# A spectral filter and a gated FFN on one core: stage A of batch 1 through folded chunks on VectorE and GpSimd, x in one lasting buffer

## The chip, the cores and the metric

The kernel runs on one core of one Trainium2 chip. The core's engines run side by side, each through its own queue of instructions in order: TensorE (PE, with its weight loads as PEld), VectorE (DVE), ScalarE (ACT), GpSimd (POOL) and the sync engine (SP). DMAs are issued from the queues of SP, ACT and POOL. The metric is the device time of one execution in microseconds (us); the span is the part of it between the first and the last recorded instruction.

## The reference, cut to what matters

```python
def _attn_ref(x, filt_r, filt_i):            # x: (8, 3008, 256) float32
    X = np.fft.rfft(x, axis=1)
    F = (filt_r + 1j * filt_i)[None, :, :]
    y = np.fft.irfft(X * F, n=x.shape[1], axis=1)
    return y.astype(np.float32)

def _moe_ref(x, w_gate, w_val, w_out):       # x: (24064, 256), d_ff 1536
    gate = np.maximum(x @ w_gate, 0.0)
    val = x @ w_val
    return (gate * val @ w_out).astype(np.float32)

# reference: _moe_ref(_attn_ref(x, filt_r, filt_i).reshape(8 * 3008, 256), w_gate, w_val, w_out)
```

Each of the 8 batches is filtered along its 3008 positions in the frequency domain, and every position then goes through a gated FFN.

## The kernel before

A transform of length 3008 is split as 94 x 32. Position s is written s = 32 n1 + n2, and a batch goes through three stages of matmuls:

- Stage A transforms over n1 for every n2. Its result goes to a DRAM buffer Abuf[b] and is gathered from there, with another order of rows, into the tile "at" (load_at, load_at_tiled).
- Stage B transforms over n2 (fwd, line 356), multiplies with the filter tiles Ftr and Fti (product, line 369, four products of 128 x 512 for each of six groups i) and transforms back (inv, line 383). Its result goes to Dbuf[b] and is read back as dC (load_d, line 423).
- Stage C transforms back over n1 and gives the FFN's input yT for a block of 512 positions (item_c, line 444; one half is copied by ScalarE, the other by VectorE).

The FFN runs over 47 blocks of 12 steps. A step multiplies with a slice of w_val and w_gate (gv, line 461: four matmuls of 512 columns, a cast vsb on ScalarE, prod on VectorE) and with a part of w_out for the block before (o_part, line 478). The stages of the coming batches are hung into these steps with at_step(s, f), which runs f in step s of the program; the order in every queue is the order of the program.

Stage A exists in two forms. The whole form (items_a, line 269) multiplies x as it is, with 94 rows of n1 in the partitions of XF, by WA in float32: 16 items of 512 columns for a batch, each with a cast on ScalarE (asb). Batches 0 and 1 use it. The folded form is for batches 2 to 7: load_chunk (line 291) brings a quarter of the batch's x into XP[j] from the GpSimd queue, once in order and once reversed; fold_chunk (line 304) forms sums and differences of rows that mirror each other, in six float32 instructions on GpSimd, two of 1024 columns and four of 512; tiled_a (line 317) multiplies them in 16 small matmuls, four at a time beside each other, and casts the result half on ScalarE and half on VectorE. A tile "fold" with two buffers holds part of a fold until its tiled_a has read it.

Ahead of the FFN stands the prologue, in this order of the program (lines 514 to 586):

- x of batch 0 is loaded into XF, the filters into Ftr and Fti from GpSimd's queue. The rows 64 to 95 of their last two groups come by loads of their own (load_own_filters, line 226).
- Stage A of batch 0 in 16 items, and the gather of at (SP's queue).
- make_back_t (line 186, casts I2t on VectorE) and make_back_u (line 199, reads I2t on TensorE, casts I2u on ScalarE) make the tables of the inverse, three calls each, with warm(6) behind each call: six matmuls on junk data, which keep TensorE busy. Between the two, place_filter(0) (line 233) copies filter rows to the partitions 32 further on, four copies of Ftr on VectorE; after them place_own, place_filter(1) and place_nyq.
- x of batch 1 is loaded into XF on SP's queue (line 557). GpSimd waits for at (hold_gpsimd, line 255: a tiny copy that holds its queue) and loads the first halves of w_val and w_gate.
- first_b (line 406) is stage B of batch 0. It calls amid(i) after each group: a short warm for i < 2, six items of batch 1's stage A after that. POOL_U (line 344) lists the products that go to GpSimd, each behind a copy xs on ScalarE.
- The spectra of batch 0 are read back, the second weight halves and w_out are loaded, the ten other items of batch 1's stage A run, and item_c(0, h) makes the first yT.

XF, WA, the junk tile and the other tiles of the pool "pro" are given up at prologue.close(); the pool "fs" of the FFN, with XP in it, takes their place. XP is cleared on GpSimd at step 2.

Of the kernel before, what the change touches and what calls it, by code (L numbers as in the profile page):

```python
# [120 lines left out]
def kernel(  # L121
# [32 lines left out]
    Abuf = [dram.tile([NROW * N2, D], BF16, name=f"Abuf{b}") for b in range(B)]  # L154
    Dbuf = [dram.tile([NROW * N2, D], BF16, name=f"Dbuf{b}") for b in range(B)]

    XF = [pro.tile([128, NX2 * D], FP32, name=f"XF{c}") for c in range(N2 // NX2)]
    WA = pro.tile([128, NROW], FP32)
    WF = consts.tile([128, 4, 32], FP32)
    M1 = consts.tile([NROW, N1], BF16)  # L160
# [79 lines left out]
    def place_nyq():  # L240
        for (src, dst), n in zip(FILT, nyq):
            nc.vector.tensor_copy(dst[96:97, NG - 1, :], n)
# [58 lines left out]
                              _ap(x, ((b * N1 + 46 + 47 * i) * N2 + 2 * j) * D,  # L301
                                  [[8 * D, 4], [-N2 * D, 32], [1, 512]]))

    def fold_chunk(b, j):

        xp = XP[j]
        t = fs.tile([128, 2, 512], FP32, tag="fold", bufs=2, name="fold")
        tt = nc.gpsimd.tensor_tensor
        tt(t, xp[:, 0:2], xp[:, 2:4], op=ALU.add)  # L309
        tt(xp[:, 2:4], xp[:, 0:2], xp[:, 2:4], op=ALU.subtract)  # L310
        tt(xp[:, 0], t[:, 0], t[:, 1], op=ALU.add)
        tt(t[:, 0], t[:, 0], t[:, 1], op=ALU.subtract)
        tt(t[:, 1], xp[:, 2], xp[:, 3], op=ALU.add)
        tt(xp[:, 2], xp[:, 2], xp[:, 3], op=ALU.subtract)
        fold[b, j] = (xp[:, 0], t[:, 0], t[:, 1], xp[:, 2])
# [25 lines left out]
                              _ap(Abuf[b], (48 * (rr % 2) + 24 * (rr // 2)) * N2 * D,  # L341
                                  [[D, 32], [N2 * D, 24], [1, D]]))

    POOL_U = ((0, 0), (0, 1), (1, 1), (2, 0), (2, 1), (3, 1), (4, 0))
    ats = {}

    def load_at(b, c):
# [159 lines left out]
    def warm(n, cols=512):  # L507

        psJ = ps.tile([128, 512], FP32, tag=fft_tag(True), name="psJ")
        for i in range(n):  # L510
            nc.tensor.matmul(psJ[:, :cols], junk[:, 0:128], junk[:, :cols], start=True, stop=True)
# [27 lines left out]
            load_at(0, 0)  # L539
    for c in range(1, 4):  # L540
        load_at(0, c)
    for i in range(3):
        make_back_t(i)
        warm(6)
    for half in range(2):
        for a in range(2):
            place_filter(0, a, half, nc.vector.tensor_copy)
    for i in range(3):
        make_back_u(i)
        warm(6)  # L550
    warm(6)
    place_own()
    for half in range(2):
        for a in range(2):
            place_filter(1, a, half, nc.vector.tensor_copy if a or not half else nc.scalar.copy)
    place_nyq()
    load_x(1, nc.sync, ((0, 0, 2 * q), (0, 2 * q, 4 * q), (1, 0, 4 * q)))

    early = items_a(1)

    def amid(i):
        if i < 2:
            warm(3, 256)
        else:
            for _ in range((1, 1, 2, 1, 1)[i - 2]):
                next(early)()

    hold_gpsimd(ats[0][0:32, NG - 1, 0:8])
    load_vg(0, DFF // 2)
    turn["tags"], turn["side"] = ("fft", "psv", "psg"), "pso"  # L570
    first_b(amid)
    turn["tags"], turn["side"] = ("fft", "psv", "psg", "pso"), None
    load_d(0, 0, 2)
    nc.gpsimd.dma_start(pro.tile([1, D], BF16, tag="last", bufs=1, name="last"),
                        _ap(Dbuf[0], (N2 * NROW - 1) * D, [[D, 1], [1, D]]))
    load_vg(DFF // 2, DFF)
    load_at(1, 0)
    for i, f in enumerate(early):
        f()
        if i == 5:  # L580
            load_at(1, 1)
    for h in range(2):
        item_c(0, h)
    hold_gpsimd(yTs[0][:, 0, 0:8])
    load_o()
    prologue.close()
    fs = ctx.enter_context(tc.tile_pool(name="fs", bufs=2))
    XP = []

    def clear_chunks():  # L590
        for i in range(4):
            XP.append(fs.tile([128, 4, 512], FP32, tag=f"XP{i}", bufs=1, name=f"XP{i}"))
            nc.gpsimd.memset(XP[i], 0.0)

    turn["tags"] = ("fft",)
    side = {}

    def at_step(s, f):
        side.setdefault(s, []).append(f)
# [1 line left out]
    for s, z in ((9, 2), (14, 3)):  # L601
        at_step(s, lambda z=z: load_d(0, z, z + 1))
    C_AT = (8, 10)
    at_step(2, clear_chunks)
    for b in range(1, B):
        end = (b * S // W - 1) * NFT + C_AT[0] - 5
        if b == 1:
            for c in range(2, 4):
                at_step(c - 2, lambda c=c: load_at(1, c))
        else:  # L610
            for j, e in enumerate((-74, -69, -64, -57)):
                l = (22, 34, 34, 46)[j] if b == 2 else end - 113 + NFT * j

                def next_x(b=b, j=j, l=l):
                    hold_gpsimd(yTs[l // NFT + 1][:, 0, 0:8])
                    load_chunk(b, j)
                    if j:
                        fold_chunk(b, j - 1)
                    if j == 3:
                        fold_chunk(b, j)  # L620
                at_step(l, next_x)
                at_step(end + e, lambda b=b, j=j: tiled_a(b, j))
            at_step(end + e + 4, lambda b=b: load_at_tiled(b))
        for i in range(7):
            l = -35 + 5 * i if b == 1 else -40 + 6 * i
            if i < 6:
                at_step(end + l, lambda b=b, i=i: fwd(b, i))
                for h in range(4):
                    at_step(end + l + h, lambda b=b, i=i, h=h: product(b, i, h // 2, h % 2))
            if i > 0:  # L630
                at_step(end + l, lambda b=b, i=i: inv(b, i - 1, ("psv", "psg")))
        at_step(end - 2, lambda b=b: load_d(b))
    prev = None
    for k in range(NB):
        prods = []
# [39 lines left out]
```

## Time and profile before

| what | value |
|---|---|
| median of 3 runs | 903.96 us (903.3 to 905.86) |
| the profiled execution | 903.85 us, of which the span is 902.1 us |
| fwd of batch 0, first matmul | 35.11 us |
| last cast of the first B ends | 53.8 us |
| first matmul of the FFN | 63.02 us |
| first matmul with w_out (block 1) | 76.22 us |

Busy time of the engines by stretch of the span, in us:

| stretch | PE | DVE | ACT | POOL | granted clock |
|---|---|---|---|---|---|
| 0 to 35 (loads, stage A of batch 0, tables) | 29.61 | 12.57 | 14.12 | 10.94 | 1.00 |
| 35 to 53.8 (first B) | 15.97 | 12.41 | 14.27 | 9.66 | 0.91 |
| 53.8 to 63 (rest of batch 1's stage A) | 8.04 | 0.69 | 6.29 | 2.02 | 1.00 |
| 63 to 76.2 (block 0) | 12.16 | 8.69 | 7.83 | 8.89 | 1.00 |
| 76.2 to 902.1 (blocks 1 to 46) | 811.33 | 534.42 | 459.61 | 327.50 | 1.00 |

The span is one execution's; the times outside it (1.75 us) are the start and the end. A line of the timeline gives the start, the length, the engine and line, the operation with its output and input, how many of it were merged, and in brackets how long the engine was idle before it and what released it. A letter q behind an engine (SPq, POOLq) stands for its queue of DMA issues.

### The profile page before, as it was taken

How to read it: one execution, taken by the hardware profiler on the slowest of the kernel's cores; microseconds unless marked ns; L12 is line 12 of the kernel's file. 1: busy time of each engine (PE TensorE's matmuls, PEld its weight loads, DVE VectorE, ACT ScalarE, POOL GpSimd, SP SyncE). 2: the span in 40 equal slices, each digit the busy share in tenths (PEclk: the TensorE clock that was granted, in tenths of full speed). 3: DMA queues.
4: the chain of work that ended last, by engine and by line, in shares of the span. 5: the costliest groups of instructions: out<-in, count | busy, mean ns of one | idle time of the engine just before them, and what ended most of it. 6: DMA issues, size and time to landing. Idle time of an engine off the chain costs nothing.

```text
span 902.1 us, 19072 instructions
## 1 busy us (share of the span) xinstructions
PE 877.1 (97%) x7089; PEld 511.1 (57%) x7210; DVE 568.8 (63%) x872; ACT 502.1 (56%) x891; POOL 359.0 (40%) x352
## 2 busy tenths in 40 slices
PE   7899999999999999999999999999999999999997
PEld 2335555566555665566655666556655566666664
DVE  2636766577765776667766677657766577655553
ACT  3475555456655555555655565655565555555552
POOL 4332398228670486515773167801868000000000
PEclk9999999999999999999999999999999999999999
DMA  9978359524465344663365434763446512321111
GB/s 248 295 204 168 106 144 188 111 81 114 137 150 123 96 132 122 143 132 105 98 162 136 107 100 105 182 126 87 112 140 148 119 30 82 90 63 36 37 34 50
DMA packets 113759, 109.18 MB, mean 121 GB/s; under 512 B 20290, under 2 KB 98370, under 8 KB 113026
## 3 DMA queue, kind: packets, MB, share of 16 engines
q1 hardware_dynamic: 90662, 80.40, 34.8%
q0 software_dynamic: 22176, 26.01, 11.9%
q10 hardware_dynamic: 828, 1.54, 0.5%
q8 instruction: 57, 0.93, 0.5%
q14 instruction: 36, 0.29, 0.1%
HBM read 61.93 MB, written 49.81 MB: 124 GB/s over the span
## 4 chain that ended last, share of the span: by engine, by line
PE 78%; POOL 5%; DMA 5%; DVE 4%; ACT 4%; issue 3%; SPq 1%; POOLq 0%; DVEq 0%
PE psG L467 24%; PE psO L486 23%; PE psV L467 22%; DVE prod L472 4%; ACT vsb L470 3%; PE psF L323 3%; PE psD L394 2%; PE psX L364 1%; DMA WgT<-in_moe_w_gate_dram 1%; PE psY L451 1%; DMA XP<-in_x_dram 1%; PE psA L276 1%; POOL XP L296 1%; DMA XF<-in_x_dram 1%; POOL fold L309 1%
## 5 line engine op out<-in xcount | busy, mean ns | idle before, releaser
L472 DVE SCALAR_TENSOR_TENSOR prod<-psG,vsb 128x512 bf16<-128x512 f32 x564 | 389.3, 690 | 265.6 <-ACT vsb L470 256.2
L470 ACT CAST vsb<-psV 128x512 bf16<-128x512 f32 x564 | 332.2, 589 | 267.8 <-PE psV L467 165.2
L467 PE MATMUL psG<-yT,WgT 128*128 128x512 bf16 x1107 | 330.8, 379 | 7.1 <-DMA WgT<-in_moe_w_gate_dram 0.6
L486 PE MATMUL psO<-WoT,prod 128*128 128x256 bf16 x2256 | 336.4, 273 | 1.1
L467 PE MATMUL psV<-yT,WvT 128*128 128x512 bf16 x1030 | 315.3, 380 | 1.2 <-ACT yT L456 1.2
L486 PEld LDWEIGHTS <-prod 128*128 128x128 bf16 x2256 | 220.6, 98 | 143.4
L467 PEld LDWEIGHTS <-WgT 128*128 128x128 bf16 x1128 | 109.9, 98 | 136.5 <-issue 2.2
L467 PEld LDWEIGHTS <-WvT 128*128 128x128 bf16 x1128 | 98.4, 98 | 42.3 <-issue 30.9
L258 POOL CAST scr<-yT 128x8 f32<-128x8 bf16 x25 | 4.7, 190 | 266.9 <-ACT yT L456 266.9
L492 ACT COPY osb<-psO 128x512 f32<-128x512 f32 x92 | 53.9, 586 | 27.4 <-PE psO L486 25.7
L380 DVE TENSOR_TENSOR tt<-psX,Ftr 128x512 bf16<-128x512 f32 x96 | 65.1, 683 | 4.6 <-PE psX L364 4.5
L309 POOL TENSOR_TENSOR fold<-XP 128x1024 f32<-128x1024 f32 x24 | 56.5, 2355 | 23.2 <-PE psF L323 23.0
L380 DVE TENSOR_TENSOR uu<-psX,Fti 128x512 bf16<-128x512 f32 x89 | 60.7, 681 | 0.0
L401 ACT CAST dsb<-psD 128x512 bf16<-128x512 f32 x96 | 51.5, 589 | 12.5 <-PE psD L394 12.4
L310 POOL TENSOR_TENSOR XP<-XP 128x1024 f32<-128x1024 f32 x24 | 56.3, 2347 | 1.9
L296 POOL DMA_DIRECT2D XP<-in_x_dram x96 | 56.2, 590 | 0.9 <-issue 0.5
L330 DVE CAST asb<-psF 128x512 bf16<-128x512 f32 x48 | 30.9, 687 | 20.5 <-PE psF L323 15.5
L330 ACT CAST asb<-psF 128x512 bf16<-128x512 f32 x48 | 25.8, 589 | 30.2 <-PE psF L323 30.2
L456 ACT CAST yT<-psY 128x512 bf16<-128x512 f32 x47 | 27.5, 586 | 24.8 <-PE psY L451 24.2
L458 DVE CAST yT<-psY 128x512 bf16<-128x512 f32 x47 | 32.0, 681 | 10.8 <-PE psY L451 10.8
L451 PE MATMUL psY<-M,dC 96*128 96x94 bf16 (+18 forms) x604 | 37.5, 198 | 0.1
L451 PEld LDWEIGHTS <-dC 96*128 96x128 bf16 x604 | 34.5, 97 | 3.6 <-issue 1.2
(66 smaller groups left out, 478.1 us busy)
## 6 DMA issues: line engine op xcount, KB each, us to landing
at<-Abuf SPq DMA_DIRECT2D x32, 384.0 KB
dC<-Dbuf SPq DMA_DIRECT2D x64, 192.0 KB
XP<-in_x_dram POOLq DMA_DIRECT2D x48, 256.0 KB, 6.0
Dbuf<-dsb SPq DMA_DIRECT2D x23, 512.0 KB
XP<-in_x_dram POOLq DMA_DIRECT2D x96, 96.0 KB, 2.7
Abuf<-asb SPq DMA_DIRECT2D x96, 96.0 KB
out_dram<-osb SPq DMA_DIRECT2D x70, 94.0 KB
XF<-in_x_dram SPq DMA_DIRECT2D x15, 256.0 KB
```

The source lines that it names most:

```text
L296: nc.gpsimd.dma_start(xp[r:r + 24, 0:4:2, :], _ap(x, (b * N1 * N2 + o) * D, [[N2 * D, 24], [47 * N2 * D, 2], [1, 512]]))
L309: tt(t, xp[:, 0:2], xp[:, 2:4], op=ALU.add)
L310: tt(xp[:, 2:4], xp[:, 0:2], xp[:, 2:4], op=ALU.subtract)
L330: copy(asf[:, :, q, :], banks[q])
L380: nc.vector.tensor_tensor(p, psX, filt, op=ALU.mult)
L401: nc.scalar.copy(dsb[:, a, o:o + 2, :], psD[a])
L451: nc.tensor.matmul(psY[:, o:o + w], dCs[b, n2 // 8][:, n2 % 8, h * 128:(h + 1) * 128], M1[:, n1:n1 + w], start=True, stop=True)
L467: nc.tensor.matmul(pt[:, :W], w[:, h, ft * 128:(ft + 1) * 128], yt[:, h, :], start=(h == 0), stop=(h == 1))
L470: nc.scalar.copy(vsb, psV[:, :W])
L472: nc.vector.scalar_tensor_tensor(prod, in0=psG[:, :W], scalar=0.0, in1=vsb, op0=ALU.max, op1=ALU.mult)
L486: nc.tensor.matmul(psO[:, t % 2], prods[ft][:, t * 128:(t + 1) * 128], WoT[:, ft, :], start=(ft == 0), stop=(ft == NFT - 1))
L492: copy(osb[:, t0 % 2:t % 2 + 1], psO[:, t0 % 2:t % 2 + 1])
```

## The change

Batch 1 takes the folded form as well. Its x is loaded into XF, which now lasts for the whole kernel: XD is XF seen as four rows of 1024 columns, and the four chunks XP[j] are views of XD. load_pairs brings two chunks at a time: the rows in order from SP's queue, the reversed rows from GpSimd's. fold_chunk takes an engine and a pool: chunks 0 and 1 of batch 1 are folded on VectorE behind the first B, chunk 2 on GpSimd at the same place, chunk 3 on GpSimd behind the loads of the weights. tiled_a(1, 0) runs ahead of the FFN, the three others in steps 1, 3 and 10 of it, and the gather of at for batch 1 in step 11. The tile "fold" moves from the pool fs to sb, with a buffer of its own in pro for chunk 0. In the prologue place_filter(0) stands ahead of make_back_t, and the seven warm(6) are together behind place_nyq. amid runs warms of 256 columns alone, POOL_U has six products instead of seven, and the clearing of XP and two holds of GpSimd's queue go. Stage B of batch 1 starts two steps later and reads back one step later.

```diff
@@ -154,7 +154,9 @@
     Abuf = [dram.tile([NROW * N2, D], BF16, name=f"Abuf{b}") for b in range(B)]
     Dbuf = [dram.tile([NROW * N2, D], BF16, name=f"Dbuf{b}") for b in range(B)]
 
-    XF = [pro.tile([128, NX2 * D], FP32, name=f"XF{c}") for c in range(N2 // NX2)]
+    XF = [consts.tile([128, NX2 * D], FP32, name=f"XF{c}") for c in range(N2 // NX2)]
+    XD = [t[:, :].rearrange("p (k n) -> p k n", k=4) for t in XF]
+    XP = [XD[j // 2][:, :, 512 * (j % 2):512 * (j % 2) + 512] for j in range(4)]
     WA = pro.tile([128, NROW], FP32)
     WF = consts.tile([128, 4, 32], FP32)
     M1 = consts.tile([NROW, N1], BF16)
@@ -301,11 +303,26 @@
                               _ap(x, ((b * N1 + 46 + 47 * i) * N2 + 2 * j) * D,
                                   [[8 * D, 4], [-N2 * D, 32], [1, 512]]))
 
-    def fold_chunk(b, j):
+    def load_pairs(b, c, ahead):
+
+        xd = XD[c]
+        if ahead:
+            for q in range(4):
+                r, o = 32 * q, 8 * q + 4 * c
+                nc.sync.dma_start(xd[r:r + 24, 0:4:2, :],
+                                  _ap(x, (b * N1 * N2 + o) * D,
+                                      [[N2 * D, 24], [47 * N2 * D, 2], [1, 1024]]))
+        else:
+            for i in range(2):
+                nc.gpsimd.dma_start(xd[:, 2 * i + 1, :],
+                                    _ap(x, ((b * N1 + 46 + 47 * i) * N2 + 4 * c) * D,
+                                        [[8 * D, 4], [-N2 * D, 32], [1, 1024]]))
+
+    def fold_chunk(b, j, eng=None, pool=None):
 
         xp = XP[j]
-        t = fs.tile([128, 2, 512], FP32, tag="fold", bufs=2, name="fold")
-        tt = nc.gpsimd.tensor_tensor
+        t = (pool or sb).tile([128, 2, 512], FP32, tag="fold", bufs=1 if pool else 2, name="fold")
+        tt = (eng or nc.gpsimd).tensor_tensor
         tt(t, xp[:, 0:2], xp[:, 2:4], op=ALU.add)
         tt(xp[:, 2:4], xp[:, 0:2], xp[:, 2:4], op=ALU.subtract)
         tt(xp[:, 0], t[:, 0], t[:, 1], op=ALU.add)
@@ -341,7 +358,7 @@
                               _ap(Abuf[b], (48 * (rr % 2) + 24 * (rr // 2)) * N2 * D,
                                   [[D, 32], [N2 * D, 24], [1, D]]))
 
-    POOL_U = ((0, 0), (0, 1), (1, 1), (2, 0), (2, 1), (3, 1), (4, 0))
+    POOL_U = ((0, 1), (1, 0), (1, 1), (2, 0), (2, 1), (3, 1))
     ats = {}
 
     def load_at(b, c):
@@ -539,59 +556,48 @@
             load_at(0, 0)
     for c in range(1, 4):
         load_at(0, c)
-    for i in range(3):
-        make_back_t(i)
-        warm(6)
     for half in range(2):
         for a in range(2):
             place_filter(0, a, half, nc.vector.tensor_copy)
     for i in range(3):
+        make_back_t(i)
+    for i in range(3):
         make_back_u(i)
+    place_filter(1, 0, 0, nc.vector.tensor_copy)
+    place_filter(1, 1, 0, nc.scalar.copy)
+    place_own()
+    place_filter(1, 0, 1, nc.vector.tensor_copy)
+    place_filter(1, 1, 1, nc.vector.tensor_copy)
+    place_nyq()
+    for i in range(7):
         warm(6)
-    warm(6)
-    place_own()
-    for half in range(2):
-        for a in range(2):
-            place_filter(1, a, half, nc.vector.tensor_copy if a or not half else nc.scalar.copy)
-    place_nyq()
-    load_x(1, nc.sync, ((0, 0, 2 * q), (0, 2 * q, 4 * q), (1, 0, 4 * q)))
-
-    early = items_a(1)
+    for c in range(2):
+        load_pairs(1, c, True)
+    hold_gpsimd(ats[0][0:32, NG - 1, 0:8])
+    for c in range(2):
+        load_pairs(1, c, False)
+    load_vg(0, DFF // 2)
+    turn["tags"] = ("fft", "psv", "psg")
+    turn["side"] = "pso"
 
     def amid(i):
-        if i < 2:
-            warm(3, 256)
-        else:
-            for _ in range((1, 1, 2, 1, 1)[i - 2]):
-                next(early)()
-
-    hold_gpsimd(ats[0][0:32, NG - 1, 0:8])
-    load_vg(0, DFF // 2)
-    turn["tags"], turn["side"] = ("fft", "psv", "psg"), "pso"
+        warm(5 if i < 2 else 4, 256)
+
     first_b(amid)
     turn["tags"], turn["side"] = ("fft", "psv", "psg", "pso"), None
     load_d(0, 0, 2)
-    nc.gpsimd.dma_start(pro.tile([1, D], BF16, tag="last", bufs=1, name="last"),
-                        _ap(Dbuf[0], (N2 * NROW - 1) * D, [[D, 1], [1, D]]))
+    for j in range(2):
+        fold_chunk(1, j, nc.vector, None if j else pro)
+    fold_chunk(1, 2)
     load_vg(DFF // 2, DFF)
-    load_at(1, 0)
-    for i, f in enumerate(early):
-        f()
-        if i == 5:
-            load_at(1, 1)
+    load_o()
+    fold_chunk(1, 3)
+    tiled_a(1, 0)
+    warm(8)
     for h in range(2):
         item_c(0, h)
-    hold_gpsimd(yTs[0][:, 0, 0:8])
-    load_o()
     prologue.close()
     fs = ctx.enter_context(tc.tile_pool(name="fs", bufs=2))
-    XP = []
-
-    def clear_chunks():
-        for i in range(4):
-            XP.append(fs.tile([128, 4, 512], FP32, tag=f"XP{i}", bufs=1, name=f"XP{i}"))
-            nc.gpsimd.memset(XP[i], 0.0)
-
     turn["tags"] = ("fft",)
     side = {}
 
@@ -601,12 +607,12 @@
     for s, z in ((9, 2), (14, 3)):
         at_step(s, lambda z=z: load_d(0, z, z + 1))
     C_AT = (8, 10)
-    at_step(2, clear_chunks)
     for b in range(1, B):
         end = (b * S // W - 1) * NFT + C_AT[0] - 5
         if b == 1:
-            for c in range(2, 4):
-                at_step(c - 2, lambda c=c: load_at(1, c))
+            for j, e in ((1, 1), (2, 3), (3, 10)):
+                at_step(e, lambda j=j: tiled_a(1, j))
+            at_step(11, lambda: load_at_tiled(1))
         else:
             for j, e in enumerate((-74, -69, -64, -57)):
                 l = (22, 34, 34, 46)[j] if b == 2 else end - 113 + NFT * j
@@ -622,14 +628,14 @@
                 at_step(end + e, lambda b=b, j=j: tiled_a(b, j))
             at_step(end + e + 4, lambda b=b: load_at_tiled(b))
         for i in range(7):
-            l = -35 + 5 * i if b == 1 else -40 + 6 * i
+            l = -33 + 5 * i if b == 1 else -40 + 6 * i
             if i < 6:
                 at_step(end + l, lambda b=b, i=i: fwd(b, i))
                 for h in range(4):
                     at_step(end + l + h, lambda b=b, i=i, h=h: product(b, i, h // 2, h % 2))
             if i > 0:
                 at_step(end + l, lambda b=b, i=i: inv(b, i - 1, ("psv", "psg")))
-        at_step(end - 2, lambda b=b: load_d(b))
+        at_step(end - (2 if b > 1 else 1), lambda b=b: load_d(b))
     prev = None
     for k in range(NB):
         prods = []
```

## The prediction

> **What bounds the kernel now.** First the page, for the bound of the whole; then the timeline of the first 65 us, since every edit but one lies there.
>
> ```profile
> PE 877.1 (97%) x7089; PEld 511.1 (57%) x7210; DVE 568.8 (63%) x872; ACT 502.1 (56%) x891; POOL 359.0 (40%) x352
> ```
>
> TensorE sets the pace once the FFN runs: between 200 and 880 us it is busy 674.4 of 680. So work that the change puts on TensorE inside the FFN costs its full length, and the place to gain is ahead of the FFN, whose first matmul comes at 63.02. The timeline of that stretch (start, length, engine, line, what):
>
> ```profile
> 24.24 0.35 PE L192 MATMUL psI<-tabs,F 64*64 64x64 bf16 x16
> 24.62 0.76 DVE L197 CAST I2t<-psI 128x256 bf16<-128x256 f32 x2 [18.28 <-PE psI L192]
> 28.77 3.87 DVE L238 COPY Ftr<-Ftr 32x3072 bf16<-32x3072 bf16 x4
> 32.42 2.75 PE L511 MATMUL psJ<-junk 128*128 128x512 bf16 x12
> 34.40 0.26 POOL L258 CAST scr<-at 32x8 f32<-32x8 bf16 x1 [11.45 <-DMA at<-Abuf]
> 35.11 0.41 PE L364 MATMUL psX<-at,F 64*64 64x256 bf16 x8
> 36.93 1.89 DVE L380 TENSOR_TENSOR tt<-psX,Ftr 128x512 bf16<-128x512 f32 x3
> ...
> 52.55 8.82 PE L276 MATMUL psA<-XF,WA 128*96 128x512 f32 x20
> ...
> 61.88 0.69 DVE L458 CAST yT<-psY 128x512 bf16<-128x512 f32 x1 [10.35 <-PE psY L451]
> ```
>
> The reader is to see that the junk matmuls end just as stage A's result of batch 0 (at) is back, 34.4, so fwd(0,0) runs at 35.11; that the first B lasts 18.7 us, to 53.8; and that ten stage A items of batch 1 (20 instructions, 8.82 us) then hold TensorE until the FFN's first psY. VectorE is idle for 10.35 us there. In the chain of waits the end of this stretch is not TensorE but a weight load:
>
> ```profile
> 52.70 1.07 ACT dsb L401 x2
> 53.80 2.41 DMA Dbuf<-dsb
> 57.78 11.67 DMA WgT<-in_moe_w_gate_dram
> ```
>
> It costs TensorE little (0.6 us until 69.50). One more answer matters, on the last filter rows (line 228) by themselves:
>
> ```profile
> L228 POOL DMA_DIRECT2D Ftr<-in_filt_r_dram x1: 591/591/591, 13.2 to 13.2; - x1
> DMA to landing us min/median/max: 15.3/15.3/15.3
> ```
>
> They land at 13.2 + 15.3 = 28.5, and the last of the four L238 copies of Ftr reads them (rows 64 to 95, groups 22 and 23).
>
> [...] after four us with TensorE mostly waiting, the clock is 0.58.
>
> ```profile
> 37.00:39.00 2.00, 0.48 (x8) 0.21 (x4) 2.00 (x4) 1.17 (x2) 0.68 (x1) 1.00 0.96 364
> 39.00:41.00 2.00, 0.81 (x14) 0.35 (x11) 2.00 (x4) 0.59 (x1) 1.88 (x3) 1.00 0.99 297
> 41.00:43.00 2.00, 2.00 (x13) 0.38 (x10) 0.21 (x1) 1.84 (x4) 1.06 (x2) 0.58 0.97 334
> ```
>
> (busy us of PE, PEld, DVE, ACT, POOL, then clock, DMA share, GB/s.) [...] each VectorE product and each prod has one input in PSUM, and beside them GpSimd's folds keep their 2341 to 2370 ns[...]. [...]
>
> **The change, part by part**, against the profiled execution: 903.85, of which 902.1 span.
>
> Prologue order. place_filter(0) moves ahead of make_back_t in VectorE's queue. Its fourth copy now waits for 28.5 and ends at 29.45; queued behind it are the six I2t casts (0.38 each), which before began at 24.62 and now end at 31.75. make_back_u on TensorE waits for them and ends at 32.3. Only then come the 42 junk matmuls, all in one block, where before they filled these very waits: 42 x 0.215 = 9.0 us (six take 1.29 in the chain), to 41.3. And TensorE has idled from 25.2 to 30.3, so I take them as starting cold: at 0.43 each (the kernel's first eleven take 4.83) for some 4.3 us, ten of them, which adds 2.1. fwd(0,0) at 43.4 instead of 35.11: 8.3 late. at is long there; GpSimd's four x loads and two weight loads (4 x 0.71 + 2 x 0.9 from 34.9, to 39.5) are hidden behind it, and SP's eight pair loads stand where nine x loads stood, behind at and long ahead of the first Dbuf write.
>
> First B. Six items of 0.87 leave TensorE, six asb casts of 0.58 leave ScalarE; warms of 0.43 to 0.53 take their place. One product moves from GpSimd to VectorE: 18 x 0.60 = 10.8. Add 0.45 for the first psX and about 1.6 of holes, while fwd(0,3) and fwd(0,4) stand behind inverses that wait for GpSimd's products (before: VectorE waited 4.1 for psX in three holes). The last product ends 12.9 after fwd(0,0), at 56.3, and with the last inverse (0.8) and its casts (1.07) B ends at 58.2; 14.8 long instead of 18.7.
>
> After the first B. The 8.82 us of psA go. VectorE gets both folds, two casts of psF and the yT cast, in this order. GpSimd starts chunk 2 after its last product, about 53.2: its ops of 2.36 run to 57.9, four of 1.27 are left. I take the exclusion as real and the two engines as alternating: VectorE waits 1.6 for the op in progress and 5.1 for the other four, and needs 9.8 itself: 72.8. Casts 1.25, yT 0.69: the FFN starts at 74.7 instead of 63.0, 11.7 late. The spectra are back before: 58.2 + 2.4 + some 5. tiled_a(1,0) and warm(8) run behind chunk 0 and end before yT even at half clock. Bounds of the exclusion: 0 (no gain is possible, nothing is taken away) and 9.8, all of chunk 2's time in front of VectorE. If GpSimd is the one that waits, its second weight half, queued behind chunk 2, is late instead: issued near 71 and landed near 82 against a need at 74, the same size.
>
> FFN. Three tiled_a, each 1.07 on TensorE (133.87 to the next psV at 134.94): +3.2, unhidden. Chunk 3 on GpSimd waits for tiled_a(1,1) to free its buffer, then takes 9.8, about when step 10 needs it; with that and a cold TensorE at the start I add 1.0 (0 to 3). The wait for WgT (-0.6) goes, as no gather of batch 1 runs beside it. Dropping the four clears of XP costs and gives nothing: GpSimd idles afterwards until 89.2. B of batch 1 two steps later: what is late next is its result before block 5, with 8 steps of 1.3 instead of 10; batch 2 lives with 9. Sum: +3.6.
>
> Total 11.7 + 3.6 = +15.3: 919.2, and as much against the median of 903.96, which is 0.1 off.
>
> **Rivals.** One: the exclusion doesn't bite. FFN start 56.3 + 9.8 + 1.94 = 68.0, +5.0 + 3.6 = 912.5. For it: nothing in this trace shows the exclusion[...]. Two: the filter rows don't hold VectorE (they land by 24), only the exclusion does. fwd(0,0) at 27.4 + 9.0 = 36.4, everything 7 earlier than forecast: 912.2. Against it: the 15.3 us[...]. Three: neither. FFN start 61.0, -2.0 + 3.2 - 0.6 + 0.3 = 904.8, no change. Four, faster: TensorE's 8.8 us go and nothing takes their place. fwd(0,0) at 36.4, B ends 51.2, the spectra are back at about 57 (2.4 and an estimated 3, as the one-row read of Dbuf took 2.9), FFN at 58.3, -4.7, and the three chunks fill the 2.0 us that block 0 wastes now (13.2 for 11.2 of matmuls): +1.2. 900.4. It decides if VectorE is through its folds by 56; the price says 59 at best.
>
> **How the numbers follow.** Forecast 0.48; rivals 0.27, 0.12, 0.07, 0.06. The forecast's own range is 914 to 923 (clock 2, exclusion 3, FFN 2). Two in ten are left out: rivals three and four below, and the ends beyond; the range is 909 to 924. About 0.3%, 2.7 us, is what can be told from no change: faster 0.06, same 0.07, slower 0.87.
>
> **What would show it.** I2t's first cast near 29.5 behind Ftr's last rows; a block of 42 psJ, partly at 0.43, and fwd(0,0) past 41; fold ops on VectorE stretched or spaced by GpSimd's; yT by VectorE as the release of the FFN. I am wrong if I2t is cast near 25, or if VectorE's twelve fold ops stand in 10 us beside GpSimd's.

## The result and the profile after

The changed kernel takes 935.51 us (median of 4, 930.01 to 936.4) against 904.91 for the kernel before (4, 903.3 to 907.4): a ratio of 1.0323, 95% interval 1.0275 to 1.0371. It is slower by 30.6 us. The forecast was 919.2, with a range of 909 to 924, so the sign was right and the size was half of it. The profiled execution took 936.4 us, of which the span is 934.4, 32.3 more than before.

The page of the changed kernel: its busy times, the clock by slices, and the chain that ended last by engine.

```profile
PE 893.9 (96%) x7338; PEld 513.5 (55%) x7338; DVE 592.4 (63%) x893; ACT 496.4 (53%) x882; POOL 377.0 (40%) x361
...
PEclk9877999999999999999999999999999999999999
...
PE 87%; DMA 8%; DVE 3%; SPq 1%; issue 1%; POOL 0%; ACT 0%; DVEq 0%; POOLq 0%
```

TensorE still sets the pace from slice 5 on. The 8% of DMA in the chain, some 75 us, and the low clock of slices 2 to 4 (23 to 93 us) say where to look: waits for transfers before and at the start of the FFN.

The timeline around the prologue's new order (start, length, engine, line, what, and in brackets the idle time before it and its releaser):

```profile
30.38 0.95 DVE L240 COPY Ftr<-Ftr 32x3072 bf16<-32x3072 bf16 x1 [4.83 <-DMA Ftr<-in_filt_r_dram]
31.37 2.08 DVE L199 CAST I2t<-psI 128x256 bf16<-128x256 f32 x6
...
33.88 11.15 PE L528 MATMUL psJ<-junk 128*128 128x512 bf16 x42
...
37.08 2.71 POOL L317 DMA_DIRECT2D XF<-in_x_dram  x4
...
44.96 0.41 PE L381 MATMUL psX<-at,F 64*64 64x256 bf16 x8
```

The filter copy waits for its rows, the I2t casts stand behind it, the 42 junk matmuls run as one block, and fwd(0,0) starts at 44.96. All of this was forecast, with 43.4 for the last. The line whose landing was not priced is the fourth: four loads of the reversed rows of x, issued from 37.08 on. The chain of waits goes through them:

```profile
37.08 25.38 DMA XF<-in_x_dram
62.46 1.65 issue
64.11 1.24 DVE fold L326
...
82.91 1.20 DVE asb L347 x2
84.11 0.61 DVE yT L475
...
84.76 0.38 PE psV L484
```

A load of 512 KB takes 25.38 us. VectorE's last product ended at 59.47 (64.11 less the 4.64 idle in the next fence). The first fold reads two of these loads; the trace has the second landing at 64.03, which is the 1.65 of "issue" in the chain, and the fold starts at 64.11. The folds on VectorE, by its timeline:

```profile
64.11 1.23 DVE L326 TENSOR_TENSOR fold<-XF 128x1024 f32<-128x1024 f32 x1 [4.64 <-issue]
...
66.63 0.69 DVE L328 TENSOR_TENSOR XF<-fold 128x512 f32<-128x512 f32 x1
67.35 2.87 DVE L329 TENSOR_TENSOR fold<-fold 128x512 f32<-128x512 f32 x1
70.26 2.71 DVE L330 TENSOR_TENSOR fold<-XF 128x512 f32<-128x512 f32 x1
```

The same instruction of 512 columns takes 0.69 with GpSimd idle and 2.87 or 2.71 from 67.34 on, when GpSimd begins chunk 2. The twelve take 64.11 to 82.91, 18.8 us.

VectorE's first yT stands at 84.03, where it was at 61.88: 22.15 of the 32.3. The other 10.2 come inside the FFN, all before block 6: VectorE's yT is 27.2 late at block 1, 30.0 at block 2, 31.8 at block 4 and 33.0 at block 6. Three places show in the chain: the three tiled_a (psF), all in block 0, with 5.1 us together; the gather of at for batch 1; and the read-back dC of its result at block 5, for which TensorE waits 3.22.

```profile
87.17 1.93 PE psF L340 x32
90.93 1.83 PE psF L340 x32
...
99.32 1.38 PE psF L340 x18
...
107.02 8.36 DMA at<-Abuf
...
169.97 10.31 DMA dC<-Dbuf
```

TensorE's longest wait for a transfer in the FFN is the one for at, in the timeline:

```profile
115.42 0.41 PE L381 MATMUL psX<-at,F 64*64 64x256 bf16 x6 [3.40 <-DMA at<-Abuf]
...
116.98 1.06 PE L503 MATMUL psO<-WoT,prod 128*128 128x256 bf16 x4
```

Batch 1's gather isn't back when its first fwd stands in the program. The wait of 3.40 costs more than itself: the pairs of matmuls behind it take up to 1.06 instead of 0.59. The granted clock was 1.00 from 109 to 115 and 0.50 from 117 to 119 (0.60 from 115.42 to 119.5), and 1.00 again from 120 on.

### The profile page after: what moved, and what is told of

Read it like the earlier page. It is cut to its first block, busy times and chain, and to the rows that moved or that the text cites. A ratio compares the mean times of both kernels' runs of the same rounds, so it can differ in the third digit from the quotient of the medians.

```text
span 934.4 us, 19485 instructions
## 1 busy us (share of the span) xinstructions
PE 893.9 (96%) x7338; PEld 513.5 (55%) x7338; DVE 592.4 (63%) x893; ACT 496.4 (53%) x882; POOL 377.0 (40%) x361
## 4 chain that ended last, share of the span: by engine, by line
PE 87%; DMA 8%; DVE 3%; SPq 1%; issue 1%; POOL 0%; ACT 0%; DVEq 0%; POOLq 0%
PE psV L484 26%; PE psG L484 26%; PE psO L503 25%; DMA XF<-in_x_dram 3%; PE psF L340 3%; PE psY L468 2%; PE psD L411 2%; DMA Ftr<-in_filt_r_dram 2%; PE psX L381 2%; DMA dC<-Dbuf 1%; DMA at<-Abuf 1%; DMA out_dram<-osb 0%; DVE fold L329 0%; DVE fold L326 0%; SPq L178 0%
## 5 line engine op out<-in xcount | busy, mean ns | idle before, releaser
L484 PE MATMUL psV<-yT,WvT 128*128 128x512 bf16 x1128 | 338.0, 381 | 4.6 <-DVE yT L475 4.2
L484 PE MATMUL psG<-yT,WgT 128*128 128x512 bf16 x1128 | 337.3, 381 | 0.3 <-DVE prod L489 0.3
L326 POOL TENSOR_TENSOR fold<-XF 128x1024 f32<-128x1024 f32 x26 | 61.2, 2354 | 39.7 <-PE psF L340 27.0
L327 POOL TENSOR_TENSOR XF<-XF 128x1024 f32<-128x1024 f32 x26 | 61.3, 2358 | 2.1
L298 POOL DMA_DIRECT2D XF<-in_x_dram x96 | 57.7, 612 | 0.6 <-issue 0.6
L347 ACT CAST asb<-psF 128x512 bf16<-128x512 f32 x56 | 30.2, 589 | 40.3 <-PE psF L340 40.3
L347 DVE CAST asb<-psF 128x512 bf16<-128x512 f32 x56 | 36.1, 686 | 19.3 <-PE psF L340 14.2
L340 PE MATMUL psF<-XF,WF 24*32 24x512 f32 x448 | 39.4, 630 | 7.0 <-ACT dsb L418 7.0
L340 PE MATMUL psF<-fold,WF 24*32 24x512 f32 x448 | 40.8, 632 | 1.8 <-DVE fold L329 1.0
```

The lines of the kernel that those rows point to most:

```text
L298: nc.gpsimd.dma_start(xp[r:r + 24, 0:4:2, :], _ap(x, (b * N1 * N2 + o) * D, [[N2 * D, 24], [47 * N2 * D, 2], [1, 512]]))
L340: nc.tensor.matmul(banks[q][32 * c:32 * c + 32], WF[r:r + 24, c, :], fold[b, j][c][r:r + 24], start=True, stop=True, tile_position=(r, 32 ...
L347: copy(asf[:, :, q, :], banks[q])
L484: nc.tensor.matmul(pt[:, :W], w[:, h, ft * 128:(ft + 1) * 128], yt[:, h, :], start=(h == 0), stop=(h == 1))
```

## The experiments

Where x loads of batch 1 are left out, the folds work on whatever stands in XF: an instruction takes the same time (1.21 to 1.23 and 0.69 without any x load in h4 and with all of them in i2), and only the transfer is missing.

**Order of the prologue put back (e1), chunk 2 left out (e2).**

```diff
# e1: place_filter(0) and the seven warm(6) where they stood before
# e2
-    fold_chunk(1, 2)
+    fold[1, 2] = tuple(XP[2][:, k] for k in range(4))
     load_vg(DFF // 2, DFF)
     load_o()
-    fold_chunk(1, 3)
...
+    hold_gpsimd(yTs[0][:, 1, 0:8])
+    fold_chunk(1, 3)
     prologue.close()
```

> The changed kernel with the prologue's order of before: warms of six between the table matmuls, the filter copies behind the I2t casts. The prediction's theory (the late start of the first B is handed on to the FFN): first fwd back to about 36 us from 44.96, the FFN 8 to 9 us earlier, about 926 in all. Rival (the folds wait for x, which lands at 62 to 64 us whatever the first B does): first fwd back at 36 as well, but VectorE's first fold still starts at 62 to 65, and the total stays within 2 us of the changed kernel's, 933 to 937.

> The changed kernel without chunk 2's six fold instructions on GpSimd (the fold of chunk 2 is left out of the computation), and chunk 3's held until the first yT is there, so that VectorE folds alone. Theory of exclusion (two-input instructions of VectorE and GpSimd shut each other out): VectorE's twelve fold instructions take 9.8 us together instead of 18.8, each 1.22 or 0.69, and the FFN starts about 9 us earlier: about 926. Rival (the folds are slowed by something else, such as the DMA traffic into the same memory): they keep stretches of 2 to 3 us and the total stays at 934 to 936.

e1: 932.14 us, ratio 1.0315 (1.0268 to 1.0363). fwd(0,0) stands at 35.65, 9.3 earlier than in the change, and the first fold at 63.12, only 1.0 earlier and again right behind its second x load (63.03). VectorE's timeline:

```profile
63.12 1.23 DVE L326 TENSOR_TENSOR fold<-XF 128x1024 f32<-128x1024 f32 x1 [10.79 <-issue]
```

VectorE now idles for 10.79 before the fold. So the late fwd(0,0), the largest term of the forecast, was real and hidden: x set the time.

e2: 935.13, ratio 1.0331 (1.0295 to 1.0368), no gain; the profiled execution is the slowest of its four, 939.18. Yet VectorE's twelve folds ran from 68.09 to 78.77, in 10.7 instead of 18.8: the exclusion is worth about 8 us there. Transfers didn't stretch the folds: in e2 253 GB/s ran from 65 to 70, and the first two folds, at 68.09 and 69.35, took 1.23 each; in the change 211 to 227 GB/s ran from 64 to 68, and the first three took 1.23, 1.22 and 0.69. Two things ate the gain. The second x load landed at 68.01, 4.0 later than in the change, and behind the folds VectorE's yT waited for the spectra, as the chain shows:

```profile
49.60 18.01 DMA Dbuf<-dsb
...
68.81 7.41 DMA Dbuf<-dsb
...
76.74 6.79 DMA dC<-Dbuf
```

Without chunk 2 in front of them on GpSimd's queue, the second weight halves were issued at 51 beside the x loads, and the first write of the spectra took 18 us. One wait went and the next stood right behind it.

**Half of the x loads left out: the reversed (e3), the ones in order (e4).**

```diff
 # e3
-    for c in range(2):
-        load_pairs(1, c, False)
 # e4
-    for c in range(2):
-        load_pairs(1, c, True)
```

> The changed kernel without the four loads of batch 1's reversed rows from GpSimd's queue (the folds of batch 1 then use the rows of batch 0 that lie there). Theory A (x of batch 1 lands at 62 to 64 us because the reversed loads are slow): the rows in order land before 45, the first fold starts right behind the last product near 59.5, the first weights land near 50, and the total falls by 4 to 6 us. Theory B (the loads of 24 rows from SP's queue are the slow ones and hold the others up): the SP loads still end past 50 and the fold starts only 0 to 3 us earlier.

> The changed kernel without the eight loads of batch 1's rows in order from SP's queue (the folds of batch 1 then use the rows of batch 0 that lie there). Theory A (the reversed loads are slow): they still take over 20 us, to about 57 or later, and the first fold gains less than 4 us. Theory B (the loads of 24 rows are slow): the reversed rows land by about 48, the fold starts right behind the last product near 59.5, and the total falls by 4 to 6 us.

e3: 925.45 (one run), the first fold at 57.08, right behind the last product. GpSimd has begun chunk 2 at 53.31 and is in its second instruction, and from there the two engines take turns. VectorE's timeline and GpSimd's:

```profile
59.20 2.17 DVE L327 TENSOR_TENSOR XF<-XF 128x1024 f32<-128x1024 f32 x1
61.41 1.63 DVE L328 TENSOR_TENSOR XF<-fold 128x512 f32<-128x512 f32 x1
```

```profile
53.31 2.35 POOL L326 TENSOR_TENSOR fold<-XF 128x1024 f32<-128x1024 f32 x1
...
58.17 2.12 POOL L328 TENSOR_TENSOR XF<-fold 128x512 f32<-128x512 f32 x1
60.37 2.12 POOL L329 TENSOR_TENSOR fold<-fold 128x512 f32<-128x512 f32 x1
```

Each instruction is recorded from the end of the one before it on its own engine, but ends only about its own length after the other engine's: GpSimd's ends at 60.29 (58.17 + 2.12), VectorE's at 61.37, 1.08 behind it, GpSimd's next at 62.49, 1.12 behind that. So both kinds last longer than alone (1.22 and 0.69 on VectorE, 1.27 for GpSimd's of 512 columns), and in these two timelines the engines shut each other out for an instruction at a time.

e4: 929.15 (one run). The reversed loads alone still take 20.3 to 20.8 us, for 25.4 to 28.1 in the change, and hold GpSimd's chunk 2; the ones in order aren't the slow ones, though the others land sooner without them.

**Why the reversed loads are slow: other forms of them (f1, f2, j1), each without the loads in order.** The line is the source's access; the destination is 128 partitions of one row of 4 KB each.

```diff
-   [[8 * D, 4], [-N2 * D, 32], [1, 1024]]     # the change: from row 46 down
+   [[N2 * D, 32], [8 * D, 4], [1, 1024]]      # f1: rows outermost, up
+   [[8 * D, 4], [N2 * D, 32], [1, 1024]]      # f2: up, else the same
+   [[40 * 1024, 4], [1024, 32], [1, 1024]]    # j1: rows next to each other
```

> As the run without the rows in order, with the reversed loads' source written with 32 rows outermost and upwards instead of 4 columns outermost and downwards (same bytes and packet size; the rows land in other partitions, so the folds of batch 1 are of other rows, and the rows in order are left out as there). Theory (the outermost count of 4[...]): the loads land in 7 to 9 us instead of 20. Rival (rows at a pitch of 32 KB in 4 KB pieces are slow to read from HBM, whatever the order): still 17 to 21 us.

> As the run without the rows in order, with the reversed loads going upwards through the same rows (4 columns outermost as before, step of the rows positive; again other rows in the folds of batch 1). Theory (the outermost count of 4): still 19 to 21 us to landing. Rival (the negative step is what is slow): 7 to 10 us.

> The kernel without the in-order loads, whose reversed loads now read four compact blocks of 32 rows of 4 KB that follow each other directly, instead of rows 32 KB apart; the destination and the order in which its partitions are written stay, and so do packets and bytes. Output of batch 1 isn't the reference's. Theory (the destination's walk sets the speed): still 18 to 21 us from issue to landing, packets near 500 ns, time near 929. Rival (the source's stride sets it): 5 to 8 us, packets near 159 ns, 925 to 927.

The time from issue to landing of the four loads (least, median, most), in e4, f1, f2 and j1 in this order:

```profile
DMA to landing us min/median/max: 20.3/20.4/20.8
```

```profile
DMA to landing us min/median/max: 4.8/5.9/7.1
```

```profile
DMA to landing us min/median/max: 18.7/20.6/20.9
```

```profile
DMA to landing us min/median/max: 12.5/14.8/16.5
```

The same 512 packets of 4096 bytes take 20.4 us or 5.9. The negative step isn't the cause (f2). Nor are there only a few packets under way: the trace's records of single packets show a median of 505 ns in e4 and 159 in f1, and in e4 512 x 505 ns in some 20 us is 13 packets at a time, over the four loads together. Each packet is slow; how many engines serve one load, no run here shows. With a source without the long stride, and else as in f2, a packet lasts 301 ns (j1): of the 346 ns between 505 and 159, 204 are gone. So one part lies in where the rows come from. The rest is open: f1 changes the order in which the source is read, and with it which row goes to which partition, while the destination's own access is the same in all four. Which of the two makes up the rest, no run here shows.

The kernel before has reversed loads of the same access with rows half as long, two for each chunk of a later batch. From its page (count, size, median to landing):

```profile
XP<-in_x_dram POOLq DMA_DIRECT2D x48, 256.0 KB, 6.0
```

They land in 6.0 us at the median and in 13.2 at most. So the order of the access alone doesn't make a load slow; whether it needs the longer rows or the four loads at once as well, no run here shows.

The times, one run each: f1 926.41, f2 929.03, j1 923.18. The kernel before took 908.21 beside the first two, 905.45 beside j1 and 906.28 beside e3 and e4, so the differences are 18.2, 20.8 and 17.7, and 19.2 and 22.9 for e3 and e4. f1's folds begin at 56.82, behind the last product, as with no reversed loads at all (e3).

**The reversed loads issued earlier (g1), and everything moved apart at once (g3).**

```diff
 # g1: the loads ahead of the hold
-    hold_gpsimd(ats[0][0:32, NG - 1, 0:8])
     for c in range(2):
         load_pairs(1, c, False)
+    hold_gpsimd(ats[0][0:32, NG - 1, 0:8])
 # g3: g1 and e1, chunks 2 and 3 on GpSimd behind yT, and
-            for j, e in ((1, 1), (2, 3), (3, 10)):
+            for j, e in ((1, 1), (2, 11), (3, 17)):
...
-            at_step(11, lambda: load_at_tiled(1))
+            at_step(18, lambda: load_at_tiled(1))
...
-            l = -33 + 5 * i if b == 1 else -40 + 6 * i
+            l = -27 + 4 * i if b == 1 else -40 + 6 * i
```

> The changed kernel with the four reversed loads ahead of GpSimd's hold on at, so issued near 25 instead of 37. Theory (the folds wait for x): x lands near 52 to 56, the first fold follows the last product at 57 to 60, Dbuf's writes are no longer held up, the FFN starts 4 to 6 us earlier: 928 to 931. Rival (something else holds the folds, or the gather of at is delayed as much by the loads beside it): 934 to 937.

> Four repairs at once: the prologue's order of before, the reversed loads ahead of the hold, chunk 2's fold on GpSimd only after VectorE's are through (held by the second half of the first yT, chunk 3 behind it), tiled_a in steps 1, 11 and 17, the gather in 18, and stage B of batch 1 from step 24 with a pitch of four steps. If slow x loads, exclusion and the late gather are the whole of the loss: first fold at 50 to 53, twelve folds in 10.7 us, FFN from 63 to 66, no wait for at over 2 us, and 909 to 914 in all, the three tiled_a (3.2 us) and a short wait for dC being what is left over before. If a large part of the loss lies elsewhere: above 918.

g1: 929.3, ratio 1.0245 (1.0201 to 1.0288), an interval that just touches the change's. g3: 941.35, ratio 1.0374 (1.0318 to 1.0429), no better than the change (the intervals overlap) where 909 to 914 was expected. The early loads run beside the gather of batch 0's stage A: fwd(0,0) stands at 49.75 in g1, where the change has 44.96, and at 48.85 in g3, where e1 has 35.65. From g3's timeline, and from its chain further on:

```profile
48.85 0.64 PE L381 MATMUL psX<-at,F 64*64 64x256 bf16 x8 [12.74 <-DMA at<-Abuf]
```

```profile
112.62 15.32 DMA at<-Abuf
```

The gather of batch 1, moved back to step 18, met the first chunk loads of batch 2, two of them reversed (issued 109.85 to 113.7), and took 15.32 instead of 8.36. That these loads are what slowed it is read from the times alone; no run takes them away. In both places tried, a load's cost came back in the transfer beside it.

**Stage B of batch 1 later and denser (h1), the three suspects of the prologue taken out (h2), both (h3).**

```diff
 # h1, h3
-            l = -33 + 5 * i if b == 1 else -40 + 6 * i
+            l = -30 + 4 * i if b == 1 else -40 + 6 * i
 # h2, h3: no load_pairs at all, e1's order, e2's chunk 2
```

> The changed kernel with one line other: stage B of batch 1 starts three steps later and its groups stand four steps apart instead of five, so that it ends three steps earlier. Theory (the 11 us between the first yT and the end are stage B of batch 1 squeezed between its gather and its read-back): TensorE's wait of 3.4 us for at before the first psX of batch 1 goes, because the gather issued in step 11 gets ten steps of 1.1 instead of seven, the half clock behind that wait goes too, and block 5 no longer waits. From block 0's yT to the end the kernel loses some 5 instead of 11, and the time is about 929 to 931. The x loads, the folds and the start of the FFN stay as they are (first yT on VectorE near 84). Rival (the eleven are the three tiled_a, the gather's traffic and the weights, wherever stage B stands): 934 to 936, with the wait for at moved to another place.

> The changed kernel with all three suspects of the prologue taken out at once: no x loads of batch 1 at all (in order and reversed both left out), the prologue's order of before, and GpSimd's fold of chunk 2 left out, that of chunk 3 held until yT. Output of batch 1 isn't the reference's. Theory (slow x loads, then the exclusion, then the order, are all there is in the prologue's loss): fwd(0,0) near 35.6, VectorE's last product near 52, twelve folds in 10.7 us right behind it, to 63, first yT of VectorE at 64 to 65, so +2 to +3 on before instead of +22; the FFN still loses some 10, and the whole is near 916 to 918. Rival (something else holds the first B or the spectra, as in the run without chunk 2, where Dbuf and dC were late): first yT at 70 or later and 922 or more.

> The run before it with stage B of batch 1 three steps later and denser as well. Output of batch 1 isn't the reference's. Theory: first yT as in that run, and from there to the end about 5 instead of 10, of which 3.2 are the three tiled_a: 911 to 913. If what is left of the FFN's loss were not the waits around stage B, it stays at 916 to 918. Below 906 only if the dropped stage A of batch 1 on TensorE is worth more than the folds on VectorE cost.

h1: 930.3, ratio 1.0268 (1.0203 to 1.0333): the first of the two expectations by its time, though its interval overlaps the change's. The wait for at is gone, the one for dC at block 5 is not: 2.92 at 174.10, for 3.22 in the change. h2: 915.67, h3: 916.61 (one run each), so no step from the one to the other, against what was expected. TensorE's longest waits from 60 to 150 in h2, then from 120 on in h3 (what waited, for what, us in total, times, the longest):

```profile
PE psY L468 <- DMA dC<-Dbuf: 4.0, 1, 4.0
PE psX L381 <- DMA at<-Abuf: 3.5, 1, 3.5
```

```profile
PE psY L468 <- DMA dC<-Dbuf: 5.9, 1, 5.9
```

The wait for at went in h3, as expected. In its place the one for dC at block 5 grew to 5.9, from 0.8 in h2: the read-back, left in its step, ran beside the last x load of batch 2 (both near 146.5). The dC wait of h2 ahead of the FFN, 3.2 in h3, is e2's: the weights are issued before the spectra are written.

**Those two mended as well (h4).**

```diff
 # h3, and
+    nc.gpsimd.dma_start(pro.tile([1, D], BF16, tag="last", bufs=1, name="last"),
+                        _ap(Dbuf[0], (N2 * NROW - 1) * D, [[D, 1], [1, D]]))
     load_vg(DFF // 2, DFF)
...
-        at_step(end - (2 if b > 1 else 1), lambda b=b: load_d(b))
+        at_step(end - (2 if b > 1 else 5), lambda b=b: load_d(b))
...                       # batch 2's last x load: step 47 for 46
```

> The run before (no x loads of batch 1, order of before, chunk 2's fold left out, stage B of batch 1 later and denser) with three lines more: the one-row read of Dbuf stands ahead of the second weight halves again, so that these start behind the first B's spectra as they did before; the read-back of batch 1's spectra is issued four steps earlier, right behind the last inverse; the last x load of batch 2 one step later. Output of batch 1 isn't the reference's. Theory (what was left of the loss there are two reads of dC, each beside transfers that overtook it: 3.2 us ahead of the FFN, where the Dbuf write took 8.4 us beside the weights, and 5.9 us at block 5): the Dbuf write takes 2 to 3 us again, first yT of VectorE at 63 to 64.5 (+1 to +2.5, the folds' own length now being what holds it), block 4 near +6, no wait for dC at block 5, end near +6 to +7: 909 to 912. Rival (the dC waits only stand in front of others, of weights or of at): first yT still near 66.5 or the end still at +12, 915 to 917.

905.52 against 904.78 (20 and 23 runs), ratio 1.0017 (0.9998 to 1.0036): the whole loss is gone, where I expected 909 to 912. VectorE's timeline in h4:

```profile
50.60 1.21 DVE L326 TENSOR_TENSOR fold<-XF 128x1024 f32<-128x1024 f32 x1
...
62.42 0.69 DVE L475 CAST yT<-psY 128x512 bf16<-128x512 f32 x1
```

The folds stand right behind the last product, take 10.6, and yT is 0.54 later than in the kernel before. This bounds what the change can reach in this order, and it leaves out a quarter of the folds and 3.5 MB of loads: no gain is in it even so.

**The two largest put back alone (i1 the exclusion, i2 the x loads), and the whole change with the rest mended (i3).**

```diff
 # i1: h4 with
-    fold[1, 2] = tuple(XP[2][:, k] for k in range(4))
+    fold_chunk(1, 2)
 # i2: h4 with all load_pairs of the change
 # i3: the change with e1's order, h3's and h4's lines; chunk 2 behind the weights on GpSimd
```

> The kernel in which everything was taken out (no x loads of batch 1, order of before, one-row read ahead of the second weight halves, stage B of batch 1 later and denser with an early read-back), with GpSimd's fold of chunk 2 put back in the change's place, behind its last product. Output of batch 1 isn't the reference's. Theory (exclusion, size as the prediction had it): GpSimd starts chunk 2 at about 47, has one or two of its six instructions done when VectorE's first fold comes at 50.6, and VectorE waits for the four or five others: its twelve folds take 15.5 to 17.5 instead of 10.6, first yT at 67 to 69 (+5 to +7), the end as much later: 910 to 913. If VectorE's two-input instructions and GpSimd's did not exclude each other, or GpSimd alone waited: folds in 10.6 to 11.5 and 905 to 907.

> The same kernel with the x loads of batch 1 put back in the change's place, in order and reversed, and chunk 2's fold left out. Output of batch 1 isn't the reference's. Theory (slow reversed loads): issued at about 36 they land at 60 to 63; VectorE's folds start there instead of at 50.6 and take 10.7, first yT at 73 to 76 (+12 to +14), and the end is as much later: 916 to 920. If the loads were slow only beside the filters, gather and weights of the change's order, they land by 52 and the time is 905 to 909.

> The changed kernel, whole, with what can be mended in the order alone: the prologue's order of before, the one-row read and the second weight halves ahead of chunk 2 on GpSimd, stage B of batch 1 three steps later and denser with its read-back right behind, chunk 3 held until yT. Theory (x loads and exclusion stand one behind the other, since GpSimd's chunk 2 also waits for x): folds from 62 to 81, first yT at 82 to 84 (+20 to +22) as in the change, and from there to the end 0 to 2 instead of 11: 925 to 928, still slower than before. If the two overlap, first yT at 78 or less and 922 or less; if the FFN's loss comes back with the whole computation, 931 or more.

| kernel | median | before | difference | VectorE's folds | first yT | span |
|---|---|---|---|---|---|---|
| h4 | 905.52 | 904.78 | +0.7 | 50.60 to 61.2 | 62.42 | 902.0 |
| i1: h4 and exclusion | 910.73 | 905.45 | +5.3 | 51.99 to 67.2 | 68.36 | 908.6 |
| i2: h4 and x loads | 918.62 | 905.45 | +13.2 | 62.09 to 72.8 | 73.89 | 916.5 |
| i3: both, whole | 924.31 | 905.45 | +18.9 | 62.12 to 78.5 | 79.57 | 922.7 |
| the change | 935.51 | 904.91 | +30.6 | 64.11 to 82.9 | 84.03 | 934.4 |

The ratios are 1.0066 (1.0032 to 1.0101) for i1, 1.0165 (1.0124 to 1.0206) for i2 and 1.0235 (1.0183 to 1.0287) for i3. The two causes come near to adding: 0.7 + 4.6 + 12.5 is 17.8, and i3 has 18.9. In part that is chance, since the exclusion in i3 isn't the meeting of i1, as GpSimd's chunk 2 stands elsewhere. GpSimd's timeline there, and VectorE's beside it:

```profile
72.77 2.38 POOL L326 TENSOR_TENSOR fold<-XF 128x1024 f32<-128x1024 f32 x1
```

```profile
71.39 4.32 DVE L330 TENSOR_TENSOR fold<-XF 128x512 f32<-128x512 f32 x1
75.74 2.71 DVE L331 TENSOR_TENSOR XF<-XF 128x512 f32<-128x512 f32 x1
```

VectorE's ten folds before that run at their own speed; GpSimd is still issuing weight loads, held behind the spectra. The last two meet chunk 2 and take 7.0 instead of 1.4. i3 is the best whole version found and is still slower than the kernel before; what remains in it is for the most part x and the exclusion (its first yT is 17.7 later, its span 20.6 longer).

## Why the prediction was wrong

- **The late fwd(0,0)**: right in every part (43.4 forecast, 44.96 measured; the junk block 9.0 + 2.1 forecast, 11.15 measured, with a granted clock of 0.50 to 36, 0.56 to 38 and 1.00 behind that) and wrong in what it was taken to cost. The forecast handed the 8.3 us on to the FFN's start; e1 takes them away and the first fold moves by 1.0.
- **The first B**: 12.9 from fwd(0,0) to the last product forecast, 14.5 measured (59.47 less 44.96). Hidden as well.
- **The step that failed** is this one: "GpSimd's four x loads and two weight loads (4 x 0.71 + 2 x 0.9 from 34.9, to 39.5) are hidden behind it". The issue was priced, 0.71 each, and the landing was put at nothing. The x loads land 25.4 to 28.1 us after their issue, behind the last product. i2 shows their worth: the first fold 11.5 later (62.09 for 50.60), 12 to 13 us in the end. None of the rivals had it, and so the range couldn't.
- **The exclusion**: right, in kind and nearly in size, though it was assumed: no trace had shown it, and the 9.8 for VectorE's twelve folds was my estimate too. Alone they take 10.6 (h4) to 10.7 (e2), at 1.21 to 1.23 for 1024 columns and 0.69 for 512. 6.7 us of waiting were forecast (1.6 + 5.1); in the change the folds take 18.8 for 10.7 alone, 8.1, and in i1, where GpSimd has a start of 3.8 us, 15.3 for 10.7, 4.6. Rival one fell.
- **"The spectra are back before"**: true in the change, though late (the psY that reads them starts at 79.54, the forecast has some 65.6), with the second weight halves behind chunk 2. Where they stood ahead of the spectra, a write took 8.4 us (h3) or 18 (e2) and became the next wait.
- **FFN, +3.6**: mis-sized, 10.2 measured (32.3 less 22.15). The three tiled_a were put at 3 x 1.07 and took 1.93, 1.83 and 1.38, 5.1 in block 0; at the first of them pairs of matmuls last 1.06, at the third 0.59 to 0.62: behind TensorE's wait of 3.78 for yT the granted clock was 0.50 from 86 to 88, and 1.00 from 90 on. In h4 they show too, with 3.0 in block 0, and by block 6 its yT is only 0.8 late and its span 0.1 shorter; waits of the kernel before are gone there (psV for ScalarE's yT 1.2, WgT 0.6, dsb 0.6), which is not all of it. Missing was the path from tiled_a(1,3) to fwd(1,0): from the last Abuf write at 103.31 to the first psX behind its gather at 115.42 are 12.1 us, while step 11 to step 18 are 7 steps of 1.3, 9.1. Named as late next, but given no cost, was batch 1's result before block 5: TensorE does wait for dC there, 3.22 at 180.41, and 5.9 in h3.
- **The sum**: 11.7 for the start of the FFN was made of 8.3 that were hidden and an exclusion that wasn't; the measured 22.15 are x (64.03 to land) and the exclusion behind it. That the kernel came out slower, as forecast, is in part luck: more than half of the forecast's 15.3 was a delay that did not reach the FFN, and the larger cause was not in it.

What isn't separated: how the 11.2 us between i3 and the change divide over the order of the prologue, stage B's start and read-back, and the place of the weights. e1 and h1 each mend one of these alone, and the intervals of both overlap the change's. The traces show only where it comes up: by VectorE's yT the change is 4.5 behind i3 at block 0, 8.5 at block 2, behind the wait for at (3.40, in i3 0.7), and 11.8 at block 6, behind the wait for dC (3.22, in i3 none).

## What to carry to other kernels

A transfer that moves to another place or takes another form has two prices, its issue and its landing. The landing is to be read in a trace from a load of the same access, size and company: here loads with the same order of access and half the size landed in 6.0 us, and four of the whole size in 20 to 28. When a suspected cost is taken out and the time stays, look in the chain for the wait that stood behind it: taking all suspects out until the loss is gone, and then putting the largest back one by one, gave prices whose sum came near the whole, where taking them out one by one did not. Folds with two inputs in SBUF, one stream on VectorE and one on GpSimd, were not parallel work merely because the queues differ: VectorE's twelve took 18.8 us beside GpSimd's six and 10.7 without them. Put such streams one behind the other, or look whether VectorE's can have an operand in PSUM: its products, which have one, kept 0.68 to 0.69 us in the kernel before, and GpSimd's folds of 1024 columns beside them 2.34 to 2.37.

## What was not expected of the hardware

Loads of 128 rows of 4 KB to 128 partitions, four of them at once, take 5.9 us each with the 32 rows outermost in the source's access and 20.4 with the four quarters outermost, at 159 and 505 ns a packet; a source of adjacent rows brings it to 14.8 and 301 ns. The last write of the spectra took 2.41 us in the kernel before and 8.38 beside the weights' loads (h3); the first, twice as large, took 4.48 in the kernel before and 18.01 beside weights and x loads (e2).
